# Weight casts as reduces, the weight difference on GpSimd, and four query pools over 128 partitions

## The chip, the cores and the metric

The kernel runs on one core of a Trainium2 chip. The metric is the device time of one execution in microseconds (us); lower is better. A core has five engines with an instruction stream each: TensorE (PE in the profile, with its weight loads as PEld), VectorE (DVE), ScalarE (ACT), GpSimd (POOL) and SyncE (SP), which issues most DMAs here. Each engine works through its own stream in order; semaphores tie the streams together.

## The reference, cut to what matters

```python
# q, k, v: 8 x 8 heads x 1152 x 64, fp32
q_pool = q.reshape(B, H, S // 2, 2, D).mean(axis=3)       # 576 queries a head
scores = scale * np.matmul(q_pool, k.transpose(0, 1, 3, 2))
scores = scores - np.max(scores, axis=-1, keepdims=True)
attn = np.exp(scores)
attn = attn / (np.sum(attn, axis=-1, keepdims=True) + 1e-09)
attn_out = np.matmul(attn, v)

x = attn_out.transpose(0, 2, 1, 3).reshape(B * S2, H * D)  # 4608 x 512
h1 = x @ w1                                                # 512 x 1024
h2 = x @ w2
out = np.maximum(h1, h2) @ w_out                           # 1024 x 512
```

## The kernel before, in words

The heads are handled in 32 pairs (`NPAIR`), four pairs to a batch. For each pair, q, k and v are loaded in fp32. GpSimd adds neighbouring queries into bf16 (`cast_q`, line 319; the factor of a half is in the scale of the exponential), and casts k (`cast_k`, line 284) and v (`cast_v`, line 326). k and the pooled q are transposed, so that the head dimension lies on partitions: for the first pairs on TensorE (`ktrans_pe`, `qtrans0`, `qtrans`) with a copy out of PSUM by VectorE (lines 395, 368, 352), for later ones by a transposing DMA issued from SP (`ktrans`, `qtrans_dma`). `K_PE` and `Q_PE` say up to which pair. Pairs 0 and 1 are pooled by VectorE over all 128 partitions (`cast_q0`, `qpf`); from pair 2 on GpSimd makes two sums of 64 partitions each, one for each head (`qp`), which lays the two heads side by side in the free dimension, so that one transpose turns both.

The scores of a pair (two heads, 576 x 1152 each) are cut into groups of 512 columns of both heads: 324 groups in all. For each group TensorE multiplies into one of three PSUM rings (`scores`, line 510), and ScalarE takes the exponential of 128 x 1024 elements into `et` (line 517). When a pair's exponentials are there, TensorE multiplies by v with a column of ones (`av_jobs`, lines 420 and 432); VectorE takes reciprocals and normalises into `xnat` (lines 442, 447, 452). When the four pairs of a batch are done, `xnat` is transposed into `xT` (TensorE for the first and the last batch, lines 572 and 578; a DMA for the others).

The MoE part uses max(h1, h2) = h2 + max(h1 - h2, 0). So it needs `wd` = w1 - w2 in bf16 (line 602), `wo` = w_out in bf16 (line 606), and `w21` = w2 @ w_out. For the last, w2 is cast to bf16 (line 599), transposed on TensorE (614, 620) and multiplied by `wo` (630, 635). Then TensorE computes `xT` by `wd` (lines 699 and 672), VectorE the maximum with 0 (708, 683), and TensorE the output by `wo` and `w21` (732, 767). The fp32 weights and their bf16 forms w2b and w2T lie for a while in buffers that `xT`, `gT` and `osb` use later.

The order of all instructions is worked out when the kernel is built, by a small planner: `Plan.op` gives every operation a cost and a due time on its engine and a modelled DMA time; the main loop picks what TensorE does next (a burst of scores, or a unit of a job from one of the queues q, k, x, a, w, p, h), and `flush` decides what is due on the other engines. `casts` holds the q, k and v casts whose loads are due, `lazy` the weight casts that VectorE makes when it is free and no q or k job is near, `line` the loads that are not yet issued, in order. `got_w` called directly issues a weight load at once, `load('w', ...)` puts it in `line`. The MoE jobs begin (`turn_at`) when the first block of `xT` and all of `wd` are due and the number of the next score group is a multiple of three; from then on scores use two of the three PSUM rings:

```python
if phase() == 1 and nxt % 3 == 0 and queue["h"]:
    turn_at[0] = nxt
    more_banks((2,))
```

Of the kernel before, what the change touches and what calls it, by code (L numbers as in the profile page):

```python
# [12 lines left out]
ALU = mybir.AluOpType  # L13

# [146 lines left out]
def bass_funnel_attn__then__act_maxout2_kernel(  # L161
# [10 lines left out]
    C, F = moe_w1.shape  # L172
# [21 lines left out]
    with ctx:  # L194
# [120 lines left out]
        def cast_q(i):  # L315
            s, r = i % 2, i % 3
            for half in range(2):
                a = qraw[r][rows(half), :, :, :]
                op("POOL", lambda g, half=half, a=a: g.tensor_tensor(  # L319
                    qp[s][:, :, half, :], a[:, :, 0, :], a[:, :, 1, :], ALU.add),  # L320
                    r=[f"qraw{r}"], w=[f"qp{s}.{half}"], after=[f"qp{s}.{1 - half}"] if i in (2, 3) else [],
                    cost=1.4, solo=half == 1)
# [16 lines left out]
        def qtrans(i):  # L339
            s = i % 2  # L340

            def go(e, m):
                mb = fb[m][:, :].bitcast(BF16)
                for u in range(QU):
                    last = e.transpose(
                        mb[:, u * HP:(u + 1) * HP],
                        qp[s][:, u, :, :].rearrange("p h d -> p (h d)"), ident[0:HP, 0:HP])
                return last
# [5 lines left out]
            return Job("q", [unit([f"qp{s}.0", f"qp{s}.1", "ident"], 0.3, go, "s")], evac, ("q", i))  # L354
# [242 lines left out]
        def w_cast(part, ct):  # L597
            if part == 0:
                dve(lambda e: e.tensor_copy(w2b[:, ct, :], w2f[:, ct, :]),
                    [f"w2f{ct}"], [f"w2b{ct}"], 0.69)  # L600
            elif part == 1:
                dve(lambda e: e.tensor_tensor(  # L602
                    wd[:, ct, :], w1f[:, ct, :], w2f[:, ct, :], ALU.subtract),
                    [f"w1f{ct}", f"w2f{ct}"], [f"wd{ct}"], 1.4)
            else:
                dve(lambda e: e.tensor_copy(
                    wo[:, 2 * ct:2 * ct + 2, :], wof[:, 2 * ct:2 * ct + 2, :]),
                    [f"wof{ct}"], [f"wo{2 * ct}", f"wo{2 * ct + 1}"], 0.69)
# [55 lines left out]
        def h_jobs(nb, tail):  # L664
# [4 lines left out]
            for ft in range(NF):  # L669
                def part(ct, ft=ft):  # L670
# [3 lines left out]
                    return unit([f"wd{ct}"] + xkeys(n0, n1), 0.216 * size / 512, go)  # L674
# [14 lines left out]
        def h_pairs(nb):  # L689
# [4 lines left out]
            for f0 in range(0, NF, 2):  # L694
                def part(ct, turn, f0=f0):
# [8 lines left out]
                    return duo([f"wd{ct}"] + xkeys(n0, n1), 0.217 * size / 512, pair, turn == 1 and ct == 0)  # L704
# [125 lines left out]
        lazy = []  # L830
        todo = []
# [9 lines left out]
        Q_PE = 5  # L841
# [39 lines left out]
        def got_w(at):  # L881
# [10 lines left out]
            later(f"{('w2f', 'w1f', 'wof')[n]}{ct}", lambda: lazy.append(ready))  # L892
# [16 lines left out]
        def flush():  # L909
# [17 lines left out]
            if lazy and plan.free.get("DVE", 0.0) <= now() and not any(  # L927
                    queue[kind] and ready_at(queue[kind][0]) <= now() + 1.5 for kind in "qk") and all(
                    j is None or j.kind not in "qk" for j in lane.values()):
                lazy.pop(0)()  # L930
            for o in list(held):
# [33 lines left out]
        def more_moe():  # L965
            tail = nxt == NGR
            step = P if tail else 2 * P
            while h_at[0] < len(hblocks):
                n0, n1 = hblocks[h_at[0]]
                keys = xkeys(n0, n1) + [f"wd{ct}" for ct in range(NC_)]  # L970
# [151 lines left out]
        part = {"a": (0, "w2f"), "b": (2, "wof"), "c": (1, "w1f")}  # L1122
        load_q(1)
        later('qraw1', lambda: (cast_q0(1,0,QU), queue['q'].append(qtrans0(1,0,QU))), margin=1.5)
        load_k(1)
        cast_k(1)
        queue['k'].extend(ktrans_pe(1))
        got_w((0, 0))
        got_w((0, 1))
        load_v(0)  # L1130
        cast_v(0)
        got_w((0, 3))
        load('w', (0, 2), got_w, 'w2f2')
        load('q', 2, load_q, 'qraw2')
        load('k', 2, load_k, 'kraw2')
        load('w', (2, 3), got_w, 'wof3')
        load('w', (2, 1), got_w, 'wof1')
        load('w', (2, 2), got_w, 'wof2')
        load('k', 3, load_k, 'kraw0')
        load('v', 1, load_v, 'vraw1')  # L1140
        load('w', (2, 0), got_w, 'wof0')
        load('q', 3, load_q, 'qraw0')
        load('w', (1, 0), got_w, 'w1f0')
        load('w', (1, 3), got_w, 'w1f3')
        load('k', 4, load_k, 'kraw1')
        load('w', (1, 2), got_w, 'w1f2')
        load('v', 2, load_v, 'vraw2')
        load('q', 4, load_q, 'qraw1')
        load('w', (1, 1), got_w, 'w1f1')
        load('v', 3, load_v, 'vraw0')  # L1150
# [120 lines left out]
```

## Time and profile before

| what | value |
|---|---|
| median of 5 runs | 382.71 us |
| lowest, highest | 380.79, 383.93 us |
| the profiled execution: own time | 380.79 us |
| its span in the trace | 379.1 us |
| granted TensorE clock | 1.00 |
| first MoE matmul (line 699) | 65.1 us |
| DMA traffic | 88.66 MB |

Busy time counts an engine's instructions in the profile, not its waits. A row of groups gives the source line, the engine, the operation, the shapes, the count, the busy time and mean duration of one, and then the idle time of the engine just before such instructions with what ended it. In a timeline, successive instructions of one line are merged: start, length, what, the count, and in brackets the idle time before the first with what ended it. The chain of waits goes back from the last instruction to what released each one. A TensorE that waits in small pieces for ScalarE still shows as mostly busy, since ends of matmuls are modelled.

### The profile page before, as it was taken

The numbers are of one execution on the slowest core, as the hardware profiler recorded it, in microseconds if no ns is written. First come the engines' busy times: TensorE is split into PE (matmuls) and PEld (weight loads), VectorE is DVE, ScalarE is ACT, GpSimd is POOL, SyncE is SP. The second block draws the span as 40 slices with busy tenths as digits, with TensorE's granted clock in tenths as the row PEclk, the third lists the DMA queues.
The fourth block names the chain that finished last, engine by engine and source line by source line (L and its number), as shares of the span: only waits on it lengthen the run. The fifth ranks groups of instructions, "written<-read, shape, count | busy, mean of one in ns | idle before, by whom it ended". The sixth has DMA issues, their size and how long they took to land.

```text
span 379.1 us, 12498 instructions
## 1 busy us (share of the span) xinstructions
PE 358.9 (95%) x5586; PEld 202.1 (53%) x5594; DVE 145.8 (38%) x304; ACT 316.3 (83%) x360; POOL 162.8 (43%) x133
## 2 busy tenths in 40 slices
PE   3889968999999999999999999998999999999996
PEld 1555545555555555554555555554655554665463
DVE  2776594342243313422442224421443145442231
ACT  4998889999999999999999999999899999811131
POOL 1356996676235740556246614654094701000000
PEclk9999999999999999999999999999999999999999
DMA  7999999999899999999799989999999974002324
GB/s 290 408 391 403 396 232 241 308 271 280 113 291 260 304 211 232 270 316 256 140 289 245 317 152 311 291 298 161 202 345 265 261 134 134 2 24 63 84 57 111
DMA packets 93542, 88.66 MB, mean 234 GB/s; under 512 B 66096, under 2 KB 66352, under 8 KB 93488
## 3 DMA queue, kind: packets, MB, share of 16 engines
q1 hardware_dynamic: 92608, 86.55, 88.3%
q10 hardware_dynamic: 880, 1.31, 0.9%
q8 instruction: 44, 0.72, 0.8%
q14 instruction: 10, 0.08, 0.1%
HBM read 62.91 MB, written 9.44 MB: 191 GB/s over the span
## 4 chain that ended last, share of the span: by engine, by line
PE 66%; ACT 22%; DMA 5%; DVE 4%; issue 1%; SPq 1%
ACT et L517 22%; PE sps L510 16%; PE fb L420 9%; PE sps L420 8%; PE fb L732 8%; PE sps L767 6%; PE sps L732 5%; DMA kraw<-in_k_dram 5%; PE sps L672 3%; PE sps L699 3%; DVE wd L602 2%; PE fb L699 2%; PE fb L432 2%; PE fb L630 1%; PE sps L432 1%
## 5 line engine op out<-in xcount | busy, mean ns | idle before, releaser
L517 ACT ACTIVATE et<-sps 128x1024 bf16<-128x1024 f32 (+1 forms) x336 | 305.2, 1017 | 18.8 <-PE sps L510 17.0
L510 PE MATMUL sps<-qpT,kT 64*128 64x256 bf16 (+7 forms) x1162 | 119.6, 289 | 4.8 <-ACT et L517 2.3
L319 POOL TENSOR_TENSOR qp<-qraw 64x576 bf16<-64x576 f32 x60 | 87.2, 1453 | 60.4 <-DMA qraw<-in_q_dram 57.9
L510 PEld LDWEIGHTS sps<-qpT,kT 64*128 64x128 bf16 x1162 | 38.6, 94 | 82.2 <-ACT et L517 67.1
L284 POOL TENSOR_SCALAR kbf<-kraw 128x1152 bf16<-128x1152 f32 x31 | 36.5, 1180 | 49.7 <-PE sps L510 39.7
L326 POOL TENSOR_SCALAR vE<-vraw 128x1152 bf16<-128x1152 f32 x32 | 37.9, 1184 | 42.0 <-DMA vraw<-in_v_dram 38.1
L420 PE MATMUL fb<-vE,et 128*128 128x65 bf16 x1368 | 48.3, 193 | 2.3 <-DVE xnat L452 2.3
L420 PEld LDWEIGHTS fb<-vE,et 128*128 128x128 bf16 x1368 | 43.5, 97 | 7.7 <-issue 4.2
L699 PE MATMUL sps<-xT,wd 64*128 64x512 bf16 (+1 forms) x240 | 35.9, 373 | 1.6 <-issue 1.0
L699 PE MATMUL fb<-xT,wd 64*128 64x512 bf16 x224 | 33.2, 376 | 0.1
L442 DVE RECIPROCAL rc<-fb 128x5 f32<-128x5 f32 (+1 forms) x38 | 7.1, 187 | 67.2 <-PE fb L420 67.2
L420 PE MATMUL sps<-vE,et 128*128 128x65 bf16 x936 | 32.8, 193 | 0.0
L732 PE MATMUL fb<-wo,stage 64*128 64x512 bf16 x224 | 32.1, 376 | 0.0
L420 PEld LDWEIGHTS sps<-vE,et 128*128 128x128 bf16 x936 | 29.8, 97 | 3.2 <-issue 2.5
L442 DVE RECIPROCAL rc<-sps 128x5 f32<-128x5 f32 (+1 forms) x26 | 4.9, 189 | 59.2 <-PE sps L420 59.2
L732 PE MATMUL sps<-wo,stage 64*128 64x512 bf16 x192 | 27.6, 376 | 0.0
L708 DVE TENSOR_SCALAR stage<-sps 128x1024 bf16<-128x1024 f32 (+1 forms) x15 | 18.1, 1205 | 18.9 <-PE sps L699 18.9
L708 DVE TENSOR_SCALAR stage<-fb 128x1024 bf16<-128x1024 f32 x14 | 17.1, 1222 | 19.9 <-PE fb L699 19.9
L767 PE MATMUL sps<-wo,stage 128*128 128x512 bf16 (+2 forms) x78 | 17.6, 357 | 0.1
L699 PEld LDWEIGHTS sps<-xT,wd 64*128 64x128 bf16 x240 | 11.2, 94 | 11.0 <-PE sps L699 1.5
L679 ACT ACTIVATE stage<-sps 128x256 bf16<-128x256 f32 (+2 forms) x12 | 4.5, 375 | 15.0 <-PE sps L672 13.7
L732 PE MATMUL fb<-w,xT 64*128 64x512 bf16 x112 | 16.6, 377 | 0.3
(70 smaller groups left out, 273.7 us busy)
## 6 DMA issues: line engine op xcount, KB each, us to landing
kraw<-in_k_dram SPq DMA_DIRECT2D x32, 576.0 KB, 7.3
vraw<-in_v_dram SPq DMA_DIRECT2D x32, 576.0 KB, 7.4
qraw<-in_q_dram SPq DMA_DIRECT2D x31, 576.0 KB, 6.8
out_dram<-stage SPq DMA_DIRECT2D x61, 128.0 KB, 2.8
xT<-in_moe_w_dram SPq DMA_DIRECT2D x4, 512.0 KB, 9.4
stage<-in_moe_w_out_dram SPq DMA_DIRECT2D x4, 512.0 KB, 14.0
stage<-in_moe_w_dram SPq DMA_DIRECT2D x4, 512.0 KB, 13.4
out_dram<-stage ACTq DMA_DIRECT2D x9, 128.0 KB, 2.6
```

The lines of the kernel that those rows point to most:

```text
L284: op("POOL", lambda g: g.tensor_scalar(kbf[s][:, :, :, :].rearrange("p t h d -> p h t d"), kraw[r][:, :, :, :], 1.0, 1.0, ALU.mult, ALU.mu ...
L319: op("POOL", lambda g, half=half, a=a: g.tensor_tensor(qp[s][:, :, half, :], a[:, :, 0, :], a[:, :, 1, :], ALU.add), r=[f"qraw{r}"], w=[f" ...
L326: op("POOL", lambda g: g.tensor_scalar(vE[r][:, :, :, 0:D].rearrange("p t h d -> p h t d"), vraw[r][:, :, :, :], 1.0, 1.0, ALU.mult, ALU.m ...
L420: last = e.matmul(fb[m][:, sb * 66:sb * 66 + 65], et[:, a:a + P], vE[vs][:, t, half, 0:65], start=(t == 0), stop=(t == NT - 1))
L432: last = e.matmul(fb[m][rows(half), NCH * 66:NCH * 66 + 65], et[:, a:a + NB], vE[vs][:, t, half, 0:65], start=(t == 0), stop=(t == NT - 1))
L442: dve(lambda e: e.reciprocal(rc[half][:, 0:n], a[:, 0:n, 64:65]), [f"f{m}"], [f"rc{half}"], 0.19)
L510: last = e.matmul(sps[r][:, h, col:col + hi - lo], kT[i % 3][rows(h), t, :], qpT[i % 3][rows(h), lo:hi], start=True, stop=True)
L517: op("ACT", lambda e: e.activation(et2[:, :, c:c + z - a], sps[r][:, :, a - g * W:z - g * W], EXP, scale=scale), r=[f"s{r}"], w=keys + [f" ...
L699: last = e.matmul(fb[m + k][:, 0:size], wd[z, ct, (f0 + k) * P:(f0 + k + 1) * P], xT[z, ct, n0:n1], start=(turn == 0 and ct == 0), stop=(t ...
L708: dve(lambda e: e.tensor_scalar_max(gT[:, f0:f0 + 2, g0:g0 + size], wide[m // 2][:, :, 0:size], 0.0), [f"f{m}", f"f{m + 1}"], w + [f"f{m}" ...
L732: last = e.matmul(fb[m + k][:, :], lhs, rhs, start=(turn == 0 and j == 0), stop=(turn == 1 and j == NC_ + NF - 1))
L767: return e.matmul(fb[m][:, 0:c1 - c0], lhs, rhs[:, c0:c1], start=(j == 0), stop=(j == NC_ + NF - 1))
```

## The change

The eight weight casts from fp32 to bf16 that VectorE made as copies (w2 and w_out) become `tensor_reduce` with max over an innermost axis of length one. The subtraction w1 - w2 goes from VectorE (four instructions of 128 x 1024) to GpSimd (eight of 128 x 512), from a list `diffs` of its own, of which `flush` takes one when GpSimd is due to be free. The pooled queries of pairs 2 to 5 are made by one GpSimd instruction over 128 partitions, and transposed with 18 TensorE transposes of 64 x 64 a pair; pair 5 was transposed by a DMA. The loads of the weights come in another order among those of q, k and v.

```diff
+AX = mybir.AxisListType
 ...
         def cast_q(i):
             s, r = i % 2, i % 3
+            if i < Q_PE:
+                op("POOL", lambda g: g.tensor_tensor(
+                    qpf[s][:, :, :], qraw[r][:, :, 0, :], qraw[r][:, :, 1, :], ALU.add),
+                    r=[f"qraw{r}"], w=[f"qp{s}.0", f"qp{s}.1"], cost=1.4)
+                return
             for half in range(2):
 ...
             def go(e, m):
                 mb = fb[m][:, :].bitcast(BF16)
                 for u in range(QU):
-                    last = e.transpose(
-                        mb[:, u * HP:(u + 1) * HP],
-                        qp[s][:, u, :, :].rearrange("p h d -> p (h d)"), ident[0:HP, 0:HP])
+                    for h in range(2):
+                        last = e.transpose(
+                            mb[rows(h), u * HP:(u + 1) * HP], qpf[s][rows(h), u, :],
+                            ident[rows(h), rows(h)])
                 return last
 ...
-            return Job("q", [unit([f"qp{s}.0", f"qp{s}.1", "ident"], 0.3, go, "s")], evac, ("q", i))
+            return Job("q", [unit([f"qp{s}.0", f"qp{s}.1", "ident"], 0.36, go, "z")], evac, ("q", i))
 ...
         def w_cast(part, ct):
             if part == 0:
-                dve(lambda e: e.tensor_copy(w2b[:, ct, :], w2f[:, ct, :]),
-                    [f"w2f{ct}"], [f"w2b{ct}"], 0.69)
-            elif part == 1:
-                dve(lambda e: e.tensor_tensor(
-                    wd[:, ct, :], w1f[:, ct, :], w2f[:, ct, :], ALU.subtract),
-                    [f"w1f{ct}", f"w2f{ct}"], [f"wd{ct}"], 1.4)
+                dve(lambda e: e.tensor_reduce(
+                    w2b[:, ct, :], w2f[:, ct, :].unsqueeze(2), AX.X, ALU.max),
+                    [f"w2f{ct}"], [f"w2b{ct}"], 1.13)
             else:
-                dve(lambda e: e.tensor_copy(
-                    wo[:, 2 * ct:2 * ct + 2, :], wof[:, 2 * ct:2 * ct + 2, :]),
-                    [f"wof{ct}"], [f"wo{2 * ct}", f"wo{2 * ct + 1}"], 0.69)
+                dve(lambda e: e.tensor_reduce(
+                    wo[:, 2 * ct:2 * ct + 2, :], wof[:, 2 * ct:2 * ct + 2, :].unsqueeze(3), AX.X, ALU.max),
+                    [f"wof{ct}"], [f"wo{2 * ct}", f"wo{2 * ct + 1}"], 1.13)
+
+        def w_diff(ct, half):
+            f0, f1 = half * F // 2, (half + 1) * F // 2
+            op("POOL", lambda g: g.tensor_tensor(
+                wd[:, ct, f0:f1], w1f[:, ct, f0:f1], w2f[:, ct, f0:f1], ALU.subtract),
+                r=[f"w1f{ct}", f"w2f{ct}"], w=[f"wd{ct}.{half}"], cost=1.25)
 ...
-        Q_PE = 5
+        Q_PE = 6
 ...
-            later(f"{('w2f', 'w1f', 'wof')[n]}{ct}", lambda: lazy.append(ready))
+            key = f"{('w2f', 'w1f', 'wof')[n]}{ct}"
+            if n == 1:
+                for half in range(2):
+                    later(key, lambda half=half: diffs.append((ct, half)))
+            else:
+                later(key, lambda: lazy.append(ready))
 ...
+            if diffs and plan.free.get("POOL", 0.0) <= now() + 0.3:
+                w_diff(*diffs.pop(0))
```

The reads of `wd` name the two halves accordingly. The loads after those of pair 0, in order (w2, w_out and w1 by their tile; those in brackets go out at once, ahead of the others, the rest from `line`):

```
before: (q1 k1 w2.0 w2.1 v0 w2.3) w2.2 q2 k2 wo.3 wo.1 wo.2 k3 v1 wo.0 q3 w1.0 w1.3 k4 w1.2 v2 q4 w1.1 v3
after:  (w2.1 q1 k1 v0 w2.2 wo.3) w2.0 q2 k2 w2.3 v1 wo.0 w1.3 wo.2 q3 k3 w1.2 wo.1 w1.0 k4 v2 q4 w1.1 v3
```

## The prediction

> **What bounds the kernel now.** I read the page's busy shares first, then the windows by stage, then the wait list and timeline of ScalarE in the first stage, and last the chain of waits there with GpSimd's and VectorE's own instructions.
>
> ```profile
> PE 358.9 (95%) x5586; PEld 202.1 (53%) x5594; DVE 145.8 (38%) x304; ACT 316.3 (83%) x360; POOL 162.8 (43%) x133
> ```
> ```profile
> 7.00:65.00 58.00, 50.28 (x846) 30.84 (x846) 39.20 (x71) 53.17 (x60) 37.78 (x26) 1.00 1.04 346
> 65.00:320.00 255.00, 251.85 (x4180) 137.90 (x4182) 87.52 (x189) 242.39 (x268) 123.35 (x97) 1.00 1.03 249
> 320.00:379.00 59.00, 55.40 (x552) 32.70 (x550) 17.78 (x40) 18.72 (x32) 0.00 (x0) 1.00 0.21 55
> ```
> Columns: stretch, length, busy PE, PEld, DVE, ACT, POOL, then clock, DMA share, GB/s. After 65 us TensorE is busy 251.85 of 255 us and carries the tail too: there is nothing to win there except by less TensorE work. Before 65 us, where no MoE matmul has begun, TensorE has 7.7 us without work, and the exponentials on ScalarE set the pace. So a microsecond in which ScalarE idles before 65 us moves the MoE start, and with it the whole dense rest, by that microsecond. ScalarE's idles there:
>
> ```profile
> 8.53 26.89 ACT L517 ACTIVATE et<-sps 128x1024 bf16<-128x1024 f32 x30 [0.17 <-PE sps L510]
> 36.63 9.27 ACT L517 ACTIVATE et<-sps 128x1024 bf16<-128x1024 f32 x10 [1.22 <-PE sps L510]
> 47.02 8.56 ACT L517 ACTIVATE et<-sps 128x512 bf16<-128x512 f32 x10 [1.11 <-PE sps L510]
> 57.18 1.02 ACT L517 ACTIVATE et<-sps 128x1024 bf16<-128x1024 f32 x1 [1.60 <-PE sps L510]
> 58.53 14.97 ACT L517 ACTIVATE et<-sps 128x1024 bf16<-128x1024 f32 x17 [0.33 <-PE sps L510]
> ```
> The brackets give the idle before each row: 1.22 + 1.11 + 1.60 + 0.33 = 4.26 us after 35 us. What is late behind each is in the chain and in GpSimd's timeline:
>
> ```profile
> 48.41 6.03 DVE wd L602 x3
> ...
> 55.07 0.43 DVE xnat L452
> 55.50 0.05 issue
> 55.55 1.27 PE fb L420 x36
> ```
> ```profile
> 30.31 3.73 POOL L319 TENSOR_TENSOR qp<-qraw 64x576 bf16<-64x576 f32 x2 [1.62 <-DMA qraw<-in_q_dram]
> ...
> 38.60 2.87 POOL L319 TENSOR_TENSOR qp<-qraw 64x576 bf16<-64x576 f32 x2 [0.31 <-DMA qraw<-in_q_dram]
> ...
> 45.81 3.13 POOL L284 TENSOR_SCALAR kbf<-kraw 128x1152 bf16<-128x1152 f32 x2
> 48.90 2.12 POOL L326 TENSOR_SCALAR vE<-vraw 128x1152 bf16<-128x1152 f32 x1
> 50.99 4.71 POOL L319 TENSOR_TENSOR qp<-qraw 64x576 bf16<-64x576 f32 x2
> ```
> Three subtractions w1 - w2 (L602) hold VectorE from 48.3 to 54.4. The normalisation of an attention block stands behind them, its PSUM bank stays taken, and TensorE waits 2.28 us for it with the next scores behind: that is the 1.60 and the 0.33. The 1.22 follows pair 3's pooled queries (GpSimd until 34.04, transposes at 35.08, evacuated by 36.01, scores at 36.20). The 1.11 precedes pair 4's first scores at 46.58, which stand behind its transposes at 43.94 and 72 attention matmuls.
>
> [...]
>
> ```profile
> L599 DVE CAST xT<-xT x4: 675/891/1907, 14.6 to 18.3; 128x1024 bf16<-128x1024 f32 x4
> L602 DVE TENSOR_TENSOR wd<-stage,xT x4: 1679/2090/2427, 44.8 to 52.0; 128x1024 bf16<-128x1024 f32 x4
> L319 POOL TENSOR_TENSOR qp<-qraw x60: 1392/1400/2366, 18.0 to 298.8; 64x576 bf16<-64x576 f32 x60
> ```
> (min/median/max ns.) A cast takes 675 alone and 1907 beside a query sum; a sum takes 1400 and up to 2366 beside the subtractions. No row here shows a reduce.
>
> **The change, part by part.**
>
> Eight weight casts (L599, L606) become reduces. Before: 4 x 1091 + 4 x 1204 ns = 9.2 us[...]. The nearest row [...]is the 128x1024 maximum out of PSUM (L708), 1222 ns; the floor is the 675 ns of a free cast. I take 1.2 us, 9.6 us in all: +0.4 us on VectorE. They hide: VectorE is busy 16.0 of the 20 us from 15 to 35 us, ScalarE idle there is under 0.1 us. Bounds: -4 us of VectorE time at the floor[...]. The gain is on GpSimd: the sums of pairs 2 and 3 lasted 3.40 and 3.73 us instead of 2.80, and this 1.5 us goes.
>
> The subtraction leaves VectorE: 4 x 2072 ns = 8.3 us gone there, and 8 half pieces arrive on GpSimd. Price: the query sum makes 576 elements in 1400 ns, 2.43 ns each, so 512 take 1.24 us; 8 x 1.24 = 9.9 us. [...] Bounds on the path: nothing if they fall into gaps, 1.24 us for each that stands in front of a needed cast. A piece also waits in order for its w1 transfer, with all k, q and v casts behind it.
>
> Queries of pairs 2 to 5: one 128-partition sum instead of two of 64. I price it at the same 1.4 us (time by elements per partition, as the k casts of 128x1152 in 1180 ns suggest; bounds 1.4 and 2.8). GpSimd saves 3.40 + 3.73 + 2.87 + 2.88 - 4 x 1.4 = 7.3 us. With the stretch from the subtractions gone too (0.83 + 0.97 + 1.9 = 3.7 us in the rows at 45.81, 48.90 and 50.99), GpSimd's load up to 61 us goes from about 36.2 to 36.2 - 7.3 - 3.7 + 9.9 = 35.1 us. It is no heavier, and pair 3's queries are ready 2.3 us sooner (3.73 - 1.4), pair 4's 1.5 us.
>
> TensorE: 18 transposes per pair in place of 9. Eighteen took 0.69 us (L361), nine 0.43 us (L345): 3 x 0.26 us, and 0.69 us for pair 5, together 1.5 us. They lie before 65 us, inside TensorE's 7.7 us. I cost them at nothing; if that cover goes, 1.5 us. Pair 5 also loses a transposing DMA (one issue of 2.22 us on SP at 49.34, about 5.7 us to landing) and gains a 0.46 us copy on VectorE, which has 8.3 us more room. SP's k transposes queue behind one issue less.
>
> Loads: the same twelve weight transfers in another order. One of 0.5 MB moves ahead of q1 and k1, at 400 GB/s 1.3 us. k1 was cast at 9.95; pair 1's scores come near 17. q3 moves up by one transfer, k3 back by three (about 4 us: cast near 30 instead of 25.5, wanted at 36). I take nothing, with up to 1.3 us against.
>
> **Sum.** Of 4.26 us, the 1.93 behind the subtractions goes whole; the 1.22 goes (2.3 us sooner), the 1.11 goes (1.5 us sooner). I take back 0.66 us, half the load delay or half a GpSimd piece in a bad place: 3.6 us. The profiled execution took 380.79 us (span 379.1 and 1.7 around it), the lowest of five, so the sum gives 377.2 against it; against the median of 382.71, **379.1**. Late next: TensorE's own work, and GpSimd's casts for pairs 5 and 6, which are wanted four microseconds sooner.
>
> **Rivals.**
>
> *More is won.* MoE may begin only when the group counter stands at a multiple of three. If attention of batch 0 comes out one turn (three groups, 2.8 us) earlier against the exponentials, TensorE's slack of that stretch is filled too, 13% by the window, at most a third by my estimate: up to 1 us more on the full 4.3, 377.4. For it: the last AV of pair 3 stood behind the subtractions. Against: the score stall ahead of it shrinks by as much.
>
> *The wait moves to GpSimd.* GpSimd was busy 9.5 and 9.8 of 10 us from 40 and 50 us. If pieces of w1 - w2 wait for their transfer, which lands near 40 us for the last, or stand before the q and k casts of pairs 4 to 6, the stall of pair 4 stays (1.11) and a piece of 1.24 us is added: 4.26 - 1.11 - 1.24 - 1.3 for q1 and k1 = 0.6, 382.1. It is also the outcome if the sums over 128 partitions take 2.8 us. Against: 13.6 us of idle on GpSimd between 10 and 40 us, when most of w1 arrives.
>
> *Slower.* The reduce is dear. Room on VectorE from 15 to 35 us is 4.0 us, 0.5 us per reduce: from 1.7 us each, copies of kT and qpT come late and ScalarE starves. At 2.3 us each the overrun is 8 x 1.1 - 4.0 = 4.8 us, more than the 4.3 won; with the load delay of 1.3 us the net is 1.8 us lost, 384.5. Above some 2.3 us the kernel is measurably slower. Against it: [...]the 1222 ns row.
>
> **Numbers.** Forecast 58%, more won 12%, moved to GpSimd 17%, slower 13%. A measurement of this kernel tells about 0.5% (1.9 us) from no change, so faster is 70%, same 17%, slower 13%. The range runs from 376.2 (everything won, and the spread of the runs shown) to 383.4, between the second and third rivals.
>
> **What would show it.** ScalarE's idle from 7 to 65 us in sum under 2 us, and no idle near 55 to 58; the first L699 near 61 instead of 65.1; reduces of one duration, 1.1 to 1.25 us; GpSimd sums at 1.4 us flat with no 2 us rows; TensorE busy still over 98% between there and the last exponential. I am wrong if the first L699 comes no sooner, if POOL's w1 - w2 pieces show waits on the moe_w1 transfers with casts behind them, or if time appears after 320 us.

## The result, and the profile after

| | before | after |
|---|---|---|
| median of the executions | 383.32 us (80) | 382.40 us (43) |
| lowest, highest | 380.45, 387.27 us | 378.54, 386.06 us |
| the profiled execution: own time, span | 380.79, 379.1 us | 380.43, 378.7 us |
| first MoE matmul | 65.1 us | 61.8 us |

The ratio after to before is 0.9953, with a 95% interval of 0.9936 to 0.997; it leaves out executions more than 1.5% above the fastest of their kernel, and so is not the quotient of the two medians. The change gains 0.47%, some 1.8 us: half of the 3.6 us that were forecast, and just inside the 0.5% that was called no change.

The busy line of the page after, and its windows by stage (columns as before: stretch, length, busy PE, PEld, DVE, ACT, POOL, clock, DMA share, GB/s):

```profile
PE 360.5 (95%) x5630; PEld 201.7 (53%) x5639; DVE 138.7 (37%) x301; ACT 316.2 (83%) x360; POOL 162.2 (43%) x137
```
```profile
7.00:65.00 58.00, 54.23 (x914) 32.18 (x919) 32.85 (x70) 53.99 (x61) 40.99 (x33) 1.00 1.07 366
65.00:320.00 255.00, 250.15 (x4164) 136.23 (x4161) 86.98 (x189) 241.82 (x268) 119.56 (x95) 1.00 1.02 244
320.00:379.00 59.00, 55.05 (x548) 32.69 (x550) 17.78 (x40) 18.38 (x31) 0.00 (x0) 1.00 0.21 55
```
TensorE has 4 us more work before 65 us, but 1.7 us less after it: MoE work came forward, and the stretch after it became looser instead of shorter. ScalarE's timeline in the first stage shows what was won (in brackets the idle time before each row):

```profile
8.79 35.14 ACT L524 ACTIVATE et<-sps 128x1024 bf16<-128x1024 f32 x39 [0.16 <-PE sps L517]
44.12 1.02 ACT L524 ACTIVATE et<-sps 128x1024 bf16<-128x1024 f32 x1 [0.18 <-PE sps L517]
47.66 13.15 ACT L524 ACTIVATE et<-sps 128x512 bf16<-128x512 f32 x15 [2.52 <-PE sps L517]
61.28 11.30 ACT L524 ACTIVATE et<-sps 128x1024 bf16<-128x1024 f32 x13 [0.47 <-PE sps L517]
```
The 1.22 us near 36 is gone. Of the 1.60 + 0.33 near 57, 0.47 is left. But the 1.11 near 47 has become 2.52. In sum the idle before the 69th exponential falls by 1.1 us, not by 3.6.

Where that 1.1 us goes later is read from ScalarE at one and the same group near 261 us and at the next idle behind it, first before, then after:

```profile
261.68 3.95 ACT L517 ACTIVATE et<-sps 128x1024 bf16<-128x1024 f32 x4 [0.31 <-PE sps L510]
266.42 5.81 ACT L517 ACTIVATE et<-sps 128x1024 bf16<-128x1024 f32 x7 [0.79 <-PE sps L510]
```
```profile
260.70 3.94 ACT L524 ACTIVATE et<-sps 128x1024 bf16<-128x1024 f32 x4 [0.31 <-PE sps L517]
266.13 5.81 ACT L524 ACTIVATE et<-sps 128x1024 bf16<-128x1024 f32 x7 [1.48 <-PE sps L517]
```
For 200 us the lead is kept (0.98 us at 261), then an idle of 1.48 instead of 0.79 takes 0.69 us back. Behind it stands TensorE's wait for batch 5's `xT`, which a DMA transposes; TensorE's timelines, before and after:

```profile
265.34 0.82 PE L699 MATMUL sps<-xT,wd 64*128 64x512 bf16 x6 [1.05 <-issue]
```
```profile
265.05 0.82 PE L709 MATMUL fb<-xT,wd 64*128 64x512 bf16 x6 [1.73 <-issue]
```
A second profile of after, below, waits only 0.45 us there, so this loss differs from execution to execution.

So the two profiled executions differ by 0.36 us, and yet the ratio says 1.8. The rest goes with the TensorE clock. The profile of before that the forecast was made from showed clock 1.00 in all its windows; of 198 executions of before that ran beside the experiments, only 14 had a mean granted clock of at least 0.9985 (median 381.4 us); 81 lay between 0.9945 and 0.9985 (383.0) and 103 lower (384.4). Of 44 executions of after, 22 reached 0.9985 (380.4 us), 19 lay between the same bounds (383.5) and 3 lower still. At the same full clock the kernels are 1.0 us apart, about the idle time that went; the rest of the 1.8 us goes with the fact that after keeps its clock more often.

How much of that the clock itself takes is not shown. A mean of 0.996 is what one stretch of 3.4 us at half clock, as in the second profile of before, leaves of 380 us, and by an estimate such a stretch holds up at most 1.7 us of matmuls: in the halved stretch of after's third profile six MoE matmuls took 1.51 us at 270.83, and 0.81 us at full clock, at 65.01. But the 19 executions of after take 3.1 us longer than those at full clock. So something else comes with it: stalls that differ between executions, or what the delay sets off further on. One such stall is on record: in a second profile of before, the idle of 1.22 us near 36 is 2.45 us, some 20 us ahead of any halving. The attention block's normalisation stands there behind three casts of w_out on VectorE, first profile and second:

```profile
29.69 3.10 DVE L606 CAST wo<-stage 128x1024 bf16<-128x1024 f32 x3
```
```profile
29.39 4.33 DVE L606 CAST wo<-stage 128x1024 bf16<-128x1024 f32 x3
```

### The profile page after: what moved, and what is told of

Same layout as the page of the kernel before. It is cut to its first block, busy times and chain, and to the rows that moved or that the text cites. A ratio compares the mean times of both kernels' runs of the same rounds, so it can differ in the third digit from the quotient of the medians.

```text
span 378.7 us, 12589 instructions
## 1 busy us (share of the span) xinstructions
PE 360.5 (95%) x5630; PEld 201.7 (53%) x5639; DVE 138.7 (37%) x301; ACT 316.2 (83%) x360; POOL 162.2 (43%) x137
## 3 DMA queue, kind: packets, MB, share of 16 engines
q10 hardware_dynamic: 880, 1.31, 0.9%
## 4 chain that ended last, share of the span: by engine, by line
PE 63%; ACT 33%; DMA 1%; issue 1%; DVE 0%; SPq 0%
ACT et L524 33%; PE sps L517 15%; PE sps L427 10%; PE sps L742 8%; PE fb L427 8%; PE sps L777 5%; PE fb L742 3%; PE fb L709 2%; PE sps L682 2%; PE sps L439 2%; PE fb L682 2%; PE fb L439 1%; PE fb L777 1%; PE sps L709 1%; PE fb L640 1%; DMA kraw<-in_k_dram 1%
## 5 line engine op out<-in xcount | busy, mean ns | idle before, releaser
L325 POOL TENSOR_TENSOR qp<-qraw 64x576 bf16<-64x576 f32 x52 | 72.8, 1400 | 60.2 <-DMA qraw<-in_q_dram 58.0
L427 PE MATMUL fb<-vE,et 128*128 128x65 bf16 x1152 | 40.7, 193 | 0.0
L427 PE MATMUL sps<-vE,et 128*128 128x65 bf16 x1152 | 40.4, 193 | 0.0
L709 PE MATMUL fb<-xT,wd 64*128 64x512 bf16 (+1 forms) x240 | 35.9, 373 | 2.0 <-issue 1.7
L709 PE MATMUL sps<-xT,wd 64*128 64x512 bf16 x224 | 33.0, 376 | 0.0
L718 DVE TENSOR_SCALAR stage<-sps 128x1024 bf16<-128x1024 f32 x14 | 17.1, 1224 | 22.3 <-PE sps L709 22.3
L718 DVE TENSOR_SCALAR stage<-fb 128x1024 bf16<-128x1024 f32 (+1 forms) x15 | 18.1, 1205 | 17.0 <-PE fb L709 17.0
L709 PEld LDWEIGHTS fb<-xT,wd 64*128 64x128 bf16 x240 | 11.2, 94 | 11.8 <-PE fb L709 2.1
L742 PE MATMUL sps<-w,xT 64*128 64x512 bf16 x112 | 16.6, 377 | 0.2
L742 PEld LDWEIGHTS sps<-wo,stage 64*128 64x128 bf16 x224 | 10.7, 94 | 8.3 <-issue 0.4
```

What stands on the lines that cost most here:

```text
L325: op("POOL", lambda g, half=half, a=a: g.tensor_tensor(qp[s][:, :, half, :], a[:, :, 0, :], a[:, :, 1, :], ALU.add), r=[f"qraw{r}"], w=[f" ...
L427: last = e.matmul(fb[m][:, sb * 66:sb * 66 + 65], et[:, a:a + P], vE[vs][:, t, half, 0:65], start=(t == 0), stop=(t == NT - 1))
L709: last = e.matmul(fb[m + k][:, 0:size], wd[z, ct, (f0 + k) * P:(f0 + k + 1) * P], xT[z, ct, n0:n1], start=(turn == 0 and ct == 0), stop=(t ...
L718: dve(lambda e: e.tensor_scalar_max(gT[:, f0:f0 + 2, g0:g0 + size], wide[m // 2][:, :, 0:size], 0.0), [f"f{m}", f"f{m + 1}"], w + [f"f{m}" ...
L742: last = e.matmul(fb[m + k][:, :], lhs, rhs, start=(turn == 0 and j == 0), stop=(turn == 1 and j == NC_ + NF - 1))
```

## The experiments

Ratios are to the kernel before, run on the same chip beside each. "Full clock" counts executions at a mean granted clock of at least 0.9985; for before it is 14 of 198. The last column counts the exponentials begun before the first MoE matmul; the planner decides some three groups ahead of it.

| kernel | ratio, 95% interval | full clock | idle of ScalarE before the 69th exponential | MoE starts at group |
|---|---|---|---|---|
| after | 0.9953 [0.9936, 0.997] | 22 of 44 | 3.34 us (before: 4.43) | 57 (before: 60) |
| before, query part alone | 0.9946 [0.9931, 0.9961] | 16 of 22 | 3.47 | 63 |
| before, subtraction part alone | 1.0026 [1.0005, 1.0048] | 7 of 22 | 4.17 | 63 |
| before, w1 copied, not subtracted | 0.9936 [0.9906, 0.9966] | 6 of 9 | 3.73 | 60 |
| after, casts as copies | 0.9951 [0.9928, 0.9975] | 13 of 22 | 3.33 | 57 |
| after, old order of loads | 1.0020 [0.9995, 1.0044] | 8 of 22 | 5.47 | 63 |
| after, short w21 matmuls | 0.9973 [0.9954, 0.9993] | 0 of 22 | 7.27 | 57 |
| after, v of pair 2 sooner, w21 held | 0.9926 [0.9890, 0.9963] | 5 of 13 | 2.13 | 63 |
| after, MoE one turn later | 0.9919 [0.9893, 0.9944] | 4 of 6 | 3.56 | 60 |
| before, some scores twice | 1.0086 [1.0054, 1.0119] | 7 of 15 | 8.56 | 60 |

**The query part alone** (before; sums of pairs 2 to 5 over 128 partitions and 18 transposes):

```diff
+            if i < Q_PE:
+                op("POOL", lambda g: g.tensor_tensor(
+                    qpf[s][:, :, :], qraw[r][:, :, 0, :], qraw[r][:, :, 1, :], ALU.add),
+                    r=[f"qraw{r}"], w=[f"qp{s}.0", f"qp{s}.1"], cost=1.4)
+                return
...
-        Q_PE = 5
+        Q_PE = 6
```


> The kernel before with only the queries of pairs 2 to 5 pooled over 128 partitions and transposed per head on TensorE. Theory: pair 3's idle of 1.22 us goes, the one before group 40 may grow, the one behind the subtractions stays; TensorE has 1.5 us more work before 65 us, which makes halved clocks rarer: full clock in more than 3 of 46 executions; ratio 0.995 to 0.999. Rival (transposes on TensorE cost what they take): ratio 1.0 to 1.004.

It gives 381.17 us, 0.9946: the whole gain of the change from one of its parts. The idles of 1.22 and 1.11 us are both gone, although the subtractions still hold VectorE; 2.31 and 0.92 us stand in their place at 54 to 66 us. So pair 4's first scores can be had in time. What after adds to this part wins the idle behind the subtractions and loses the one at group 40 again.

**The subtraction part alone** (before; w1 - w2 as eight GpSimd pieces from `diffs`):

```diff
-            elif part == 1:
-                dve(lambda e: e.tensor_tensor(
-                    wd[:, ct, :], w1f[:, ct, :], w2f[:, ct, :], ALU.subtract),
-                    [f"w1f{ct}", f"w2f{ct}"], [f"wd{ct}"], 1.4)
...
+            if diffs and plan.free.get("POOL", 0.0) <= now() + 0.3:
+                w_diff(*diffs.pop(0))
```


> The kernel before with only the subtraction moved to GpSimd in eight pieces (the planner moves other work in turn, MoE begins four groups later than before). Theory (VectorE's subtractions caused 1.93 us of idle, the rest of the gain is the clock): the idle at 57 us goes, GpSimd rows are not stretched after 44 us, but pairs 3 and 4 keep their waits; ratio 0.996 to 1.0. Rival (the move alone is the gain): 0.994 or below.

384.08 us, 1.0026: no gain. The 1.60 and 0.33 us go, 1.23 and 1.11 stay, and the MoE work starts three groups later, at 63. In its trace TensorE, which has little but scores until then, loses its clock at 66.2 us, and an idle of 1.59 us follows on ScalarE at 70. From the last exponential to the end this kernel needs 1.8 us more than before, as does every kernel here that starts at 63.

**The subtraction made free** (before; w1 copied into `wd`, w2 left out of it, so the output is another; same order on every engine):

```diff
-                dve(lambda e: e.tensor_tensor(
-                    wd[:, ct, :], w1f[:, ct, :], w2f[:, ct, :], ALU.subtract),
+                dve(lambda e: e.tensor_copy(wd[:, ct, :], w1f[:, ct, :]),
```


> The kernel before with w1 copied into wd in place of the subtraction (w2 left out of it), planner cost kept, so the order is the same; VectorE's rows there fall from about 2.07 to 0.7 to 1.2 us. If the subtractions on VectorE are what holds the normalisation of pair 3: the 1.60 and 0.33 us idles at 57 and 58 go, the end comes 1.5 to 2 us sooner than before (ratio 0.995). Rival (given back in the dense stage): ratio 0.998 to 1.0 although the idles go.

380.12 us, 0.9936. The two idles behind the subtractions are gone, which shows that they did stand behind VectorE, as the prediction read it; 6 of 9 executions are at full clock. In its trace the idle near 36 is 1.93 us instead of 1.22, behind a halved clock from 28.5 us; the ratio is no worse than that of the whole change.

**The casts as copies again** (after, same order):

```diff
-                dve(lambda e: e.tensor_reduce(
-                    w2b[:, ct, :], w2f[:, ct, :].unsqueeze(2), AX.X, ALU.max),
+                dve(lambda e: e.tensor_copy(w2b[:, ct, :], w2f[:, ct, :]),
```


> The changed kernel with the eight weight casts as tensor_copy again, planner costs kept, so the order is the same. [...] copies of 0.68 us alone, up to 1.9 us beside GpSimd work, GpSimd rows stretched by 1 to 3 us in sum up to 35 us (casts of k, sums, w1 - w2 pieces), end 0 to 1 us later than the changed kernel. Rival (reduces do nothing for GpSimd): GpSimd rows at 1.15, 1.25 and 1.42 us as they are.

381.29 us, 0.9951, against 0.9953: the reduces are worth nothing at the end. w2's copies take 0.68 us and w_out's 1.20, where all eight reduces take 1.21. GpSimd's rows beside the copies are longer by some 1.1 us in sum, and nothing waited for them. This holds for after alone: the second profile of before shows copies of w_out that did hold up TensorE.

**The old order of loads** (after):

```diff
-        load('w', (0, 0), got_w, 'w2f0')
-        got_w((0, 1))
         load_q(1)
...
+        got_w((0, 0))
+        got_w((0, 1))
         load_v(0)
...
```


> The changed kernel with the old order of loads. The MoE start then falls after 62 groups. Theory: MoE is 14 or more matmuls behind at the 200th exponential and the tail is 50.5 instead of 48.7 us; early idle under 4 us; ratio 0.998 to 1.004: the load order is needed only to keep the start at or under 60 groups. Rival (the load order is the main gain by itself, by q3 and v0 arriving sooner): idle over 5 us before the 69th exponential.

384.96 us, 1.0020. Idles of 1.31 and 2.44 us at 44 to 56, and a start at 63 groups. The order of the loads, which the forecast counted as "nothing to 1.3 us against", is what brings the new work to its places in time. The kernel's plan follows from it, so this run doesn't separate a late transfer from a changed order on TensorE.

**What holds group 40: the length of w2 @ w_out** (after, with 64 of 512 columns multiplied and repeated into `w21`, so the output is another; same order):

```diff
-                        return e.matmul(fb[m][:, :], w2T[:, ct, ft, :], wo[:, ft, :],
+                        return e.matmul(fb[m][:, 0:64], w2T[:, ct, ft, :], wo[:, ft, 0:64],
```


> The changed kernel with each w2 @ w_out matmul cut from 512 to 64 columns (so w21 is not the reference's; 64 columns repeated), same order of instructions. Theory 1 (ScalarE's 2.52 us idle before group 40 comes from TensorE, which still has w21 and the 72 attention matmuls of pair 2 ahead of those scores): some 28 matmuls save 0.15 us each before 44 us, scores of group 40 come 2.5 to 4 us sooner, the idle falls under 0.7 us, and the end comes 2 to 3 us sooner than the changed kernel (ratio to before about 0.988). Rival A (the stall waits for pair 4's pooled queries): the idle stays above 2 us. Rival B (idle goes, but the gain is given back in the dense stage): ratio to before stays at 0.993 to 0.996.

382.42 us, 0.9973, and the idle before group 40 grew to 4.31 us. The windows of its trace say why the run doesn't answer the question:

```profile
35.00:40.00 5.00, 3.19 (x43) 1.54 (x41) 2.15 (x4) 5.00 (x7) 4.79 (x5) 1.00 1.04 406
40.00:45.00 5.00, 3.79 (x30) 1.81 (x31) 1.68 (x3) 5.00 (x7) 4.96 (x5) 0.53 1.04 397
```
With less work TensorE was busy 3.19 of 5 us, and at 40.3 its clock was halved for 10.2 us (0.53 in the second row). None of its 22 executions had a full clock.

**What holds group 40: pair 2's attention block** (after, with v of pair 2 loaded two transfers sooner, ahead of a part of w1 and of k of pair 4, and w2 @ w_out held until that block is issued):

```diff
+                if kind == "w" and len(queue["w"] and queue["w"][0].units) == NF and av_half.get(2) != 2:
+                    continue
...
         load('w', (2, 1), got_w, 'wof1')
+        load('v', 2, load_v, 'vraw2')
         load('w', (1, 0), got_w, 'w1f0')
         load('k', 4, load_k, 'kraw1')
-        load('v', 2, load_v, 'vraw2')
```


> The changed kernel with v of pair 2 loaded three transfers sooner and the w2 @ w_out matmuls held until the attention product of pair 2 is issued. Theory (group 40's scores stand behind the 3.2 us block of pair 2's attention product, which the planner put directly in front of them, since the exponentials' buffer holds two pairs): the block comes earlier with score groups on both sides, the 2.52 us idle falls under 0.8 us, the 69th exponential ends 1.5 to 2.5 us sooner. MoE then starts after 62 groups instead of 56, which cost 1.8 us of tail in the two kernels where it did, so the end comes within 1 us of the changed kernel (ratio 0.993 to 0.998). Rival (pair 4's pooled queries or its k hold group 40): the idle stays above 1.5 us.

380.59 us, 0.9926. ScalarE's timeline has no idle at group 40 any more:

```profile
8.34 45.42 ACT L524 ACTIVATE et<-sps 128x1024 bf16<-128x1024 f32 x51 [0.16 <-PE sps L517]
54.74 9.51 ACT L524 ACTIVATE et<-sps 128x1024 bf16<-128x1024 f32 x10 [0.98 <-PE sps L517]
```
TensorE's timeline of after has pair 2's block right ahead of the scores in question:

```profile
44.00 0.47 PE L352 MATMUL fb<-ident,qp 64*64 64x64 bf16 x18
44.53 0.47 PE L439 MATMUL fb<-vE,et 128*64 128x65 bf16 x18
44.94 2.35 PE L427 MATMUL fb<-vE,et 128*128 128x65 bf16 x72
47.22 0.61 PE L517 MATMUL sps<-qpT,kT 64*128 64x256 bf16 x8
```
The transposes of pair 4's queries at 44.00 are no bound: GpSimd had those queries at 40.18 (at 41.47 before), the transposes stood at 43.94 before, and VectorE had copied their result at 44.98, 2.2 us ahead of these scores. What the scores wait for is the row of 72 matmuls. Group 40 holds pair 4's first scores, and `et` holds two pairs, so pair 2's must be read first. Which of the two edits moved the block ahead of its need isn't told apart. The first 69 exponentials end 1.2 to 1.6 us sooner than in profiles of after, and 1.8 us are lost at the end, as in every kernel here that starts the MoE work at 63 groups.

**The earlier start of the MoE work** (after, held to 60 exponentials, as before; the planner's counter `nxt` stands at 57 then):

```diff
+        HOLD = 57
...
-            if phase() == 1 and nxt % 3 == 0 and queue["h"]:
+            if phase() == 1 and nxt % 3 == 0 and queue["h"] and nxt >= HOLD:
```


> The changed kernel with the MoE start held back by one turn of three score groups (first MoE matmul after as many groups as in the kernel before). If the earlier start is worth what I put on it, the end comes 0.5 to 1 us later than the changed kernel. Rival (the lead of some 16 MoE matmuls is used up where MoE work runs out before the next batch's attention is done): within 0.3 us of the changed kernel.

379.55 us, 0.9919: not slower. After leads by 16 MoE matmuls at the 69th exponential (56 against 40), and by the 200th both have 254 + 288. A turn's lead is worth nothing up to 60 groups.

**More profiles of both kernels**, to see whether the first ones were typical.

> The kernel before once more, for a second profile. Of the 46 timed executions so far only 3 show a full mean clock, so a profile with a mean clock near 0.995 is likely. Theory (TensorE's clock is halved for a few microseconds where it was little busy just before): the halved stretch lies before 65 us, where MoE has not begun, and ScalarE idles longer than the 4.26 us of the first profile. Rival (the lower clock comes at any place, whatever TensorE does): the stretch lies after 65 us, or anywhere.

> The changed kernel once more, for a second profile; about half of its executions show a mean clock of 0.996, at 383.5 us instead of 380.4. Theory: the halved stretch lies before 65 us, in a part where TensorE itself is late, so that it costs 3 us. Rival: it lies in the dense stage, where TensorE bounds, and costs its length there.

> The changed kernel for a third profile, to see where its halved clock lies, which costs it 3.1 us (383.5 against 380.4) where it costs the kernel before about 0.8. Theory: in the block of 44 to 47 us or right after it, where TensorE is late already, or in the first dense microseconds after 60 us. Rival: near 15 us, where TensorE has room, and the 3 us have another cause.

The second profile of before (383.26 us) has a halved clock from 58.1 for 3.4 us, right behind the stall at the subtractions, and idles of 2.45, 1.11, 1.75, 0.96 and 0.46 us. The second of after has full clock (378.97 us), not the halved stretch that was expected; its wait for batch 5 is 0.45 us. The third took 385.72 us: its wait is 3.09 us, and the clock is halved from 266.6 for 6.8 us, not in the first stage, where it was expected. With a mean of 0.989 it is lower than all 44 executions above, so it doesn't stand for the common case of one lost stretch. Its TensorE timeline, and the window that ends where the clock falls:

```profile
267.46 1.47 PE L709 MATMUL fb<-xT,wd 64*128 64x512 bf16 x6 [3.09 <-issue]
```
```profile
263.19:266.60 3.41, 1.18 (x19) 0.52 (x15) 0.85 (x3) 2.44 (x3) 0.29 (x1) 1.00 1.10 119
```

**More matmuls to keep the clock up** (before; the score matmuls of groups 24 to 35 and 48 to 56 issued twice):

```diff
-                for i, t, lo, hi, col in pieces(g):
+                for i, t, lo, hi, col in [x for x in pieces(g) for _ in range(2 if 24 <= g < 36 or 48 <= g < 57 else 1)]:
```


> The kernel before with the score matmuls of groups 24 to 35 and 48 to 56 issued twice into the same place (same result, same order, some 0.22 us more TensorE work for each of 21 groups, 4.6 us in all, before 65 us). Theory (TensorE's clock is halved for 3.4 us after a stretch in which it was little busy): full mean clock in at least a third of the executions instead of 7 of 89, and the end 0.5 to 1.5 us sooner in spite of the added work (ratio 0.996 to 0.999). Rival (the clock has nothing to do with the work; added work delays each score group): clocks as before, ratio 1.002 to 1.01.

386.68 us, 1.0086. Full clocks became more frequent (7 of 15, against 1 of 43 for before beside it), but the added work delays the scores by more than the clock returns: at full clock it still takes 385.3 us.

**The wait for batch 5's transpose, taken away by SP's order.** Four kernels issue pair 26's key transpose six microseconds later, so that the five transposes of `xT` stand ahead of it; no other engine's order changes by it. They are after, before, after with the start at 60, and after with v of pair 2 sooner and w21 held.

```diff
-                later(f"kbf{i % 2}", lambda: (ktrans(i), k_hi.update({i: NT})), ("k", i))
+                later(f"kbf{i % 2}", lambda: (ktrans(i), k_hi.update({i: NT})), ("k", i), 6.0 if i == 26 else 0.0)
```


> After, with one key transpose (pair 26) issued six microseconds later, so that the five transposing DMAs of batch 5's attention output stand ahead of it on SP's queue; the other engines' orders are unchanged. Theory (the wait for this transfer at 264 us gives back part of the gain and starts the halved clock of the dense stage): the wait there, 1.73 and 3.09 us in two profiles of after, falls below 0.5 us; executions at mean clock above 0.9985 rise from 22 of 44 to three quarters or more; median near 380.5, ratio 0.991 to 0.993. Rival (the clock halves for another reason and the wait is covered): ratio as after, 0.995, and the share of full-clock executions stays at half. Second rival: the key transpose is late instead, a new stall at pair 26, 383.

> Before, with the same single key transpose issued later. Theory: before loses its clock early, at the stall behind the subtractions at 58 us, so the transfer of batch 5 moves it by 1 us at the most: ratio 0.997 to 1.000, full-clock executions stay rare (under a quarter). Rival (the transfer is what costs before its clock): 0.990 to 0.993, most executions at full clock.

> After with the later MoE start (60 groups) and batch 5's transfer ahead of pair 26's key transpose. Theory: the later start costs nothing and the wait at 264 us goes: as the kernel with the transfer moved alone, within 0.3 %, ratio 0.990 to 0.993. Rival: the two moves are not independent, 0.995 or above.

> After with v of pair 2 loaded three transfers sooner, w2@w_out held back, and batch 5's transfer ahead of pair 26's key transpose. Theory: the first stage is 1.3 us shorter, the tail 1.8 us longer (50.5), the wait at 264 us was not there: 380 to 381, ratio 0.992 to 0.994, no better than without the move of the transfer. Rival (the wait was there in most executions): 379 or below, ratio 0.989.

| kernel | median | ratio, 95% interval | full clock |
|---|---|---|---|
| after, key transpose later | 382.13 us | 0.9957 [0.9928, 0.9986] | 10 of 22 |
| before, key transpose later | 383.91 us | 0.9991 [0.9965, 1.0017] | 3 of 22 |
| after, start at 60, key transpose later | 378.56 us | 0.9863 [0.9816, 0.9909] | 6 of 6 |
| after, v of pair 2 sooner, w21 held, key transpose later | 380.44 us | 0.9911 [0.9887, 0.9935] | 6 of 18 |

The first did not do what it meant to: its wait is 2.49 us. SP's timeline, of after and of this kernel:

```profile
256.81 6.95 SPq L565 DMA_TRANSPOSE xT<-xnat  x5
```
```profile
253.40 10.07 SPq L565 DMA_TRANSPOSE xT<-xnat  x5
```
The transposes began 3.4 us sooner and took 3.1 us longer. SP's order had let the loads of q and k of a later pair, 576 KB each, in ahead of them. In before the move misses in the same way: three loads went ahead, the transposes took 10.94 us, and the wait grew from 1.05 to 1.96 us. So its ratio, though as expected, doesn't tell what the wait is worth in before. In the kernel with the start at 60 the wait is gone; the one with v of pair 2 sooner had none to begin with.

**The loads held back too** (after, and after with the start at 60):

```diff
-            while line and plan.dma_free - now() < DEPTH and plan.when("SP", w=[line[0][3]]) <= now() + 0.6:
+            while line and not (26 in k_began and 5 not in x_sent) and plan.dma_free - now() < DEPTH and plan.when("SP", w=[line[0][3]]) <= now() + 0.6:
```


> After, with pair 26's key transpose and also the loads of v, q and k (576 KB each) held back until batch 5's five transposing DMAs are issued; only SP's queue differs. The kernel that held the key transpose alone let two of these loads in ahead, and its five transposes took 10.07 us instead of 6.95, so its wait (2.49 us) did not shorten. Theory (DMA traffic ahead of the transposes makes the wait at 264 us): they start near 253, take under 7.5 us, the wait falls below 0.5 us, three quarters of executions at full clock, ratio 0.990 to 0.993. Rival (the late transfer only goes with the halved clock): ratio as after, 0.995, the full-clock share stays at half. Second rival: the loads held back come late for pairs 27 to 29 and stall, 382 or more.

> The same hold in after with the MoE start at 60 groups. Theory that the later start by itself brings after below 380 in nearly every execution (9 of 12 so far at full clock): 378.5 to 379.6, ratio 0.986 to 0.991, with no wait for batch 5 longer than 0.3 us. Rival (the kernels with this start were lucky in few executions): half the executions below full clock, ratio 0.994 or above.

After alone: 379.56 us, 0.9913 [0.9878, 0.9947], 6 of 6 executions at full clock (378.4 to 380.55). SP and TensorE in its trace:

```profile
254.06 7.64 SPq L565 DMA_TRANSPOSE xT<-xnat  x5
```
```profile
264.83 0.81 PE L709 MATMUL fb<-xT,wd 64*128 64x512 bf16 x6
```
The transposes take 7.64 us, and no idle stands before the MoE matmuls. Six in a row would come up in 1.6% of cases if half were at full clock still. In this profile, of the slowest of the six, ScalarE's idle behind the 200th exponential (7.46 us) is no smaller than in after's first (7.53): what the wait itself took comes back at other groups, and TensorE idles 1.47 us ahead of output matmuls at 247.7, where after did not. So a good part of the gain is the clock, but not all: among executions at full clock this kernel's median of 379.6 is 0.8 us below the 380.4 of after, and that is not explained here.

After with the start at 60 and this hold: 378.11 us (377.94 to 379.08), 0.988 [0.9845, 0.9915]: the best version here with the one before it (378.56), faster than both kernels of the change.

## Why the prediction was right or wrong, point by point

**The bound.** Right for the first 260 us: 1.1 us less of ScalarE's idle moved the exponentials by 0.98 us at 261. Wrong behind it: "the whole dense rest" doesn't follow. A wait for a transposing DMA at 264 us, which the prediction did not look for, took 0.69 us of it back in the profiles compared.

**The casts as reduces.** Right in price: 1.206 to 1.209 us against 1.2. The 1.5 us on GpSimd that they were to save went to nothing that waited: put back as copies in after, they change nothing, though the four sums over 128 partitions took 1544 ns in the mean in that kernel and 1411 in after. Why they take longer beside the copies was not shown. What the prediction did not see is that the copies of before vary: three of w_out took 3.10 us in one profile and 4.33 in the other, with TensorE behind them.

**The subtraction on GpSimd.** Right in price: eight pieces in 10.1 us against 9.9, and no row of the sums is stretched any more: those over 128 partitions take 1402 to 1417 ns, those over 64 take 1392 to 1409, where before had up to 2366. The rows by form of GpSimd before 65 us:

```profile
L616 POOL TENSOR_TENSOR wd<-stage,xT 128x512 bf16<-128x512 f32 x8 | 10.1, 1270 | 1.8 <-DMA stage<-in_moe_w_dram 1.5
L319 POOL TENSOR_TENSOR qp<-qraw 128x576 bf16<-128x576 f32 x4 | 5.6, 1411 | 4.5 <-DMA qraw<-in_q_dram 4.5
```
The rival in which pieces block GpSimd waiting for w1 did not come: 1.5 us of waiting in all. Of the 1.93 us "that goes whole", 0.47 stayed.

**The sum over 128 partitions.** Right: 1.41 us. Pair 3's queries are ready at 29.82 us instead of 34.04, and the 1.22 is gone.

**The transposes on TensorE.** Eighteen take 0.47 us; counted at nothing. Pair 4's lie just ahead of the block that group 40 waits behind, and cost no more there than the nine did (0.43).

**The loads.** They were counted only as a delay, of nothing to 1.3 us. The run with the old order is 0.7% above after, with a start six groups later. What they decide is the order of TensorE's work.

**The sum. Here the forecast failed.** The term is "the 1.11 goes (1.5 us sooner)". The queries did come 1.3 us sooner; the wait was not for them. The prediction named the 72 attention matmuls ahead of those scores and then credited the gain to the queries alone. With ScalarE earlier and TensorE's block 0.6 us later, the term measured 2.52 us: 1.4 us lost where 1.1 was to be won, 2.5 us of a sum of 3.6. The reserve of 0.66 did not cover it. The part with the queries alone shows the term can go, and the kernel with v of pair 2 sooner shows it going within after. That the ratio still gives 1.8 us, and not the 1.1 of the idle or the 0.36 between the two profiles, goes with the clock, which the forecast left out: that part was luck.

**The base.** The 3.6 us were taken from a profile at full clock, the lowest of five, and set against the median as if the two differed by noise. They differ in clock, 14 of 198 executions of before being like that profile, and in stalls such as the 2.45 us near 36. That error worked the other way: where the clock falls behind it, 3.4 us at half clock come on top of the stall at 53 to 58 us, as in the second profile of before; what they cost in time was not measured alone. The windows of that stretch, before and after:

```profile
53.00:58.00 5.00, 2.31 (x52) 1.71 (x48) 3.63 (x9) 3.40 (x4) 4.83 (x4) 1.00 0.84 207
```
```profile
53.00:58.00 5.00, 4.66 (x78) 2.92 (x79) 2.96 (x8) 5.00 (x7) 4.18 (x4) 1.00 1.28 215
```
TensorE's weak stretch of before is filled in after. In two other traces with before's order on TensorE, the second profile of before and before with the key transpose later, this same stretch was followed by the halved clock, at 58.1 and 56.9 us.

**The rivals.** "More is won" rested on an earlier turn: the turn came (57 instead of 60), and is worth nothing. "The wait moves to GpSimd" and "slower" did not come, and the 2.3 us a reduce that the latter priced was the author's assumption (they took 1.21); 382.4 us was reached for another reason than the 382.1 of the former. The signs that the text gave: the first L709 at 61.8 ("near 61"), reduces of one duration, sums flat at 1.4 were all met, and TensorE was 98.1% busy behind 65 us ("over 98%"); "idle under 2 us" was not.

**What stays open.** Why after with the start at 60 keeps its clock in 15 of 18 executions (three kernels together) was not tried: it has another order on TensorE from 60 groups on, and no wait for batch 5 in the two profiles with a later key transpose, but 1.14 us for it and 1.70 us for batch 3 in the one without. Nor is it shown which stall costs after its clock in most executions. One trace has the halving behind the wait at 264 us. Waits of 1.73, 1.95 and 2.49 us there, in after and in the kernels with the casts as copies and with the key transpose later, were not followed by one; and that last kernel and after with the start at 60 lost their clock at 16 to 17 us, in work that they share with after.

## What to carry to other kernels

When a wait ends last, read which instruction stands directly ahead of the late one on its own engine: an input that comes sooner wins nothing if the engine is on another block of work then, as pair 4's queries, 1.3 us sooner, won nothing here. Before summing gains against one profile, check that its clock is that of the median execution; a stall that leaves TensorE half idle for a few microseconds can be followed by 3.4 us at half clock, as in the second profile of before, where it was busy 1.47 of 3.41 us. And follow a gain to the end of the kernel: compare the same group's start every hundred microseconds, and see at which wait the lead is lost.

## What the runs showed of the hardware

The granted clock fell to 0.5 in stretches of 3.4 us (second profile of before, at 58.1), 6.8 us (third of after, at 266.6) or 10.2 us (after with short w21 matmuls, at 40.3): one length, twice and three times. Cut each of the 20 traces of these kernels into windows of 3.41 us, counted from the points where its own clock changes: of 2056 windows at full clock ahead of 370 us, 12 were followed by a halving, and TensorE was busy between 1.02 and 2.08 us in each of them. Only 8 of the others were as low (1.59 to 2.03 us). So of the 20 windows in which TensorE was busy for at most 2.08 us, 12 were followed by a halving and 8 were not; matmul ends are modelled and some records missing, so the bound is rough. The window ahead of the halving in the second profile of before:

```profile
54.70:58.11 3.41, 1.47 (x40) 1.25 (x40) 2.57 (x7) 1.81 (x2) 3.41 (x3) 1.00 0.92 242
```
In the first profile of before the bounds of such windows, at 51.48, 54.90 and 58.31, cut the same stall in two, with TensorE busy 1.74 us (one of the 8) and 2.35, and the clock stayed. Why one kernel loses its clock in some executions only was not shown.

So taking work from TensorE need not save time: leaving out seven eighths of w2 @ w_out took the full clock from all 22 executions (1.84 of 3.41 us busy ahead of the halving in its trace), at a ratio of 0.9973 against 0.9953 with all of it, and adding matmuls raised the share at full clock from 1 of 43 to 7 of 15.

The clock records of a trace begin only 9 to 23 us into the span, mostly near 14, and matmuls were slower before that: four score matmuls of 64 x 256 took 0.61 us at 6.69 us in the first profile of before, and 0.39 at 17.85. The 1.00 of a view doesn't show this, and "full clock" leaves it out.

Five transposing DMAs took 6.95 to 8.41 us with the same data in the traces of before and after, and 10.07 and 10.94 us behind two and three loads of 576 KB on the queue (after and before with the key transpose later). They took 9.54 us in the kernel with v of pair 2 sooner and the key transpose later, where the last two loads went out 3.6 and 3.0 us ahead of them, so what sets their time was not shown by this alone.

In after a GpSimd sum took 1.40 us for 64 x 576 and 1.41 us for 128 x 576: twice the partitions at the same time. The subtraction of 128 x 512 took 1.27 us.
